# Local attention and two MLPs on one core: dilated rows in 1 KB runs, early clears on VectorE, filler products from a tile of their own up to the third slot

## The chip, the core and the metric

The kernel runs on one core of a Trainium2 chip. The core has TensorE (PE in the rows, its weight loads PEld), VectorE (DVE), ScalarE (ACT), GpSimd (POOL) and SyncE (SP), each with an instruction queue that is worked off in order, and 16 DMA engines. The metric is the device time of one execution in microseconds, as the median of several runs. Beside these there is one profiled execution, from which all rows are.

## The reference

```python
# q, k, v: (4, 8, 576, 64) float32; window 32, dilation 4
scores = q @ k.T / 8
rel = pos[:, None] - pos[None, :]
mask_plain = (rel >= 0) & (rel < 32)                        # heads 0 to 3
mask_dil = (rel >= 0) & (rel < 128) & (rel % 4 == 0)        # heads 4 to 7
attn = softmax(where(mask, scores, -1e9)); x = attn @ v     # x: 2304 tokens x 512
h = x @ w_in1;  x = max(0.01 * h, h) @ w_out1               # 512 -> 2048 -> 512
h = x @ w_in2;  out = softplus(h) @ w_out2
```

## The kernel before

The tokens are cut into eight windows `w` of 288 (half a sequence each), the heads into four pairs `p`: pairs 0 and 1 are plain, 2 and 3 dilated. A dilated head is worked as four residues modulo 4, since a query sees only keys of its own residue. One pair of one window is an object `Pair`; below, "pair n" counts them over windows, so pairs 0 to 3 are window 0 and pairs 4 to 7 window 1. These eight are *early*: their q and k come as token rows (`load_rows`), are turned by TensorE (`pe_trans`), copied out by ScalarE (`evac_k`, `evac_q`), multiplied (`scores_early`, with the mask added as a bf16 product of `ident_b` and `masks_b`), copied to SBUF by ScalarE (`scores_copy`), reduced over keys by GpSimd (`rowmax`, about 2 us each), then `less_max` on VectorE, `exp` on ScalarE, `pv` on TensorE (two halves for a dilated pair), `inv` on VectorE, `xT` on TensorE, `x_hi` on ScalarE and `x_lo` on VectorE, which leave the first MLP's input as two float32r parts. Early pairs borrow SBUF from weight tiles that are filled later. One piece `f` of the weights (128 of 2048 hidden columns, 1 MB) needs `rebias`, `low`, `split_hi` on ScalarE and `shift`, `join`, `add`, `split_lo` on VectorE before TensorE may use it.

The first MLP runs in slots: a slot is `g1` (12 products into a bank `h`) for one token block and one `f`, and, two slots later, `g2`. Slots 0, 1 and 2 are block 0 (256 tokens of window 0) with f = 0, 1, 2; slot 3 is block 1 (tokens 256 to 511) with f = 0, for which pairs 4 to 7 must be done. Its last three products need the channels of pair 7.

All instructions are written out in an order that a list scheduler in the program makes (`run_schedule`): every step has an engine, a cost and due time, and the written order is then fixed for each engine. Into the order of TensorE it puts *spins*: products that nobody reads, three of 288 columns a group, into bank `y3` (cost 0.37 in the plan, after a start of 3.2 in the plan's own time). Each group takes the bank anew, and its first product waits for TensorE's own last one. A spin is put in where TensorE has nothing ready (or, by `FILL`, ahead of a step that has just come ready); with the first `g1` they end. A spin that stands in the order runs: it holds TensorE for its length whether or not the next step is ready.

SP issues nearly all DMAs in the order of the plan; its transfers go through one queue in the order of issue. At the start GpSimd makes identity and masks (`setup`), clears the eight borrowed tiles of the early pairs (8 memsets, `clear`) and then the later pairs' `kt`, `qz` and `v` (6 memsets); VectorE casts the masks to bf16, and the first spin reads that cast.

## Time and profile before

| what | value |
|---|---|
| median of 3 runs (lowest, highest) | 930.68 us (930.04, 933.78) |
| the profiled execution's own time | 932.96 us |
| its span in the trace | 930.9 us |
| TensorE busy with products | 911.4 us (98%) |
| VectorE busy | 650.3 us (70%) |
| ScalarE busy | 460.8 us (50%) |
| GpSimd busy | 74.8 us (8%) |

In the rows, a line of the timeline is start, duration, engine, source line, operation, output from input, shapes and count, and in square brackets the idle time before it and what ended that. A row of a table of stretches has, in this order: the stretch, its length, the busy time and number of instructions of TensorE, of its weight loads, of VectorE, ScalarE and GpSimd, the granted TensorE clock as a share of full speed (2.4 GHz), the mean busy share of the DMA engines, and what they moved in GB/s.

### The profile page before, as it was taken

The page shows a single profiled execution, that of the slowest core. Times are in us where ns is not written, and L with a number is a line of the kernel's source. Part 1 is how long each engine was busy: PE and PEld are TensorE (multiplying, and loading weights), DVE is VectorE, ACT ScalarE, POOL GpSimd, SP SyncE. Part 2 cuts the span into 40 slices and gives each one's busy share as a digit, 9 for nine tenths or more (in the row PEclk, how much of TensorE's full clock was granted, in tenths as well). Part 3 has the DMA queues.
Part 4 walks back from the last instruction along what each step waited for, and adds up shares of the span by engine and source line. Part 5 has one row for each costly group of instructions (what it writes and reads, how often), then busy time and mean ns, then how long its engine had stood idle before and what let it go on. Part 6 is the DMA issues. An engine that isn't in the chain of part 4 may idle for free.

```text
span 930.9 us, 15804 instructions
## 1 busy us (share of the span) xinstructions
PE 911.4 (98%) x6047; PEld 862.2 (93%) x6048; DVE 650.3 (70%) x1276; ACT 460.8 (50%) x935; POOL 74.8 (8%) x57
## 2 busy tenths in 40 slices
PE   6989999999999999999999999999999999999998
PEld 4889999999999999999999988989899999989896
DVE  4989994475664765747546777877877777777775
ACT  3768753334434443443456744554645545444543
POOL 5500030010110201201100000000000000000000
PEclk9879999999999999999999999999999999999999
DMA  9887123254463644542358500200200000000000
GB/s 230 216 249 256 21 43 69 69 138 120 101 159 94 151 105 130 130 125 86 98 167 281 180 1 1 68 1 1 68 1 0 35 1 1 35 1 1 35 1 34
DMA packets 139902, 81.50 MB, mean 88 GB/s; under 512 B 101172, under 2 KB 124724, under 8 KB 139828
## 3 DMA queue, kind: packets, MB, share of 16 engines
q1 hardware_dynamic: 137428, 79.92, 30.4%
q8 instruction: 47, 0.77, 0.4%
q10 hardware_dynamic: 2400, 0.59, 0.3%
q14 instruction: 27, 0.22, 0.1%
HBM read 62.65 MB, written 17.83 MB: 86 GB/s over the span
## 4 chain that ended last, share of the span: by engine, by line
PE 93%; DVE 2%; ACT 1%; DMA 1%; issue 0%; SPq 0%; DVEq 0%
PE h L679 43%; PE yp L722 22%; PE yo L818 21%; PE pv L611 3%; PE sc L562 3%; PE xt L632 1%; DMA y<-ys 1%; DVE cf L281 0%; DVE w L311 0%; PE sc L535 0%; DVE lent L590 0%; PE spin L386 0%; DVE ln L795 0%; DVE ln L791 0%; DVE gl L805 0%
## 5 line engine op out<-in xcount | busy, mean ns | idle before, releaser
L679 PE MATMUL h<-xh,w 128*128 128x384 f32 (+3 forms) x1792 | 443.9, 317 | 0.7 <-DVE w L311 0.7
L679 PEld LDWEIGHTS h<-xh,w 128*128 128x128 f32 x1792 | 313.7, 189 | 5.5 <-DVE w L311 1.2
L679 PE MATMUL h<-xl,w 128*128 128x384 f32 (+3 forms) x896 | 281.5, 314 | 0.0
L722 PE MATMUL yp<-gh,w 128*128 128x288 f32 (+2 forms) x1024 | 229.0, 299 | 0.9 <-DVE ys L732 0.9
L818 PE MATMUL yo<-w,gh 128*128 128x512 f32 x576 | 180.4, 394 | 0.3 <-ACT gh L801 0.3
L679 PEld LDWEIGHTS h<-xl,w 128*128 128x128 f32 x896 | 169.5, 189 | 4.3
L722 PEld LDWEIGHTS yp<-gh,w 128*128 128x128 f32 x1024 | 171.5, 188 | 1.2 <-DVE ys L732 1.2
L722 PE MATMUL yp<-gl,w 128*128 128x288 f32 (+2 forms) x512 | 150.8, 295 | 0.0
L775 ACT ACTIVATE hc<-h 128x384 f32<-128x384 f32 x96 | 47.1, 490 | 179.6 <-PE h L679 179.5
L695 ACT ACTIVATE hc<-h 128x288 f32<-128x288 f32 (+2 forms) x128 | 52.2, 408 | 168.1 <-PE h L679 166.0
L818 PEld LDWEIGHTS yo<-w,gh 128*128 128x128 f32 x576 | 106.9, 188 | 18.5 <-ACT gh L801 1.4
L818 PE MATMUL yo<-w,gl 128*128 128x512 f32 x288 | 114.5, 398 | 0.3 <-DVE gl L805 0.3
L704 DVE TENSOR_TENSOR gl<-hc,gh 128x288 fp32r<-128x288 f32 (+2 forms) x128 | 58.4, 456 | 54.9 <-ACT gh L700 54.2
L722 PEld LDWEIGHTS yp<-gl,w 128*128 128x128 f32 x512 | 96.2, 188 | 0.1
L786 DVE TENSOR_SCALAR z<-hc 128x384 f32<-128x384 f32 x96 | 34.5, 359 | 75.7 <-ACT hc L776 75.7
L586 POOL PARTITION_ALL_REDUCE mx<-s x24 | 49.4, 2058 | 354.3 <-DVE s L576 354.3
L818 PEld LDWEIGHTS yo<-w,gl 128*128 128x128 f32 x288 | 54.1, 188 | 14.1 <-DVE gl L805 1.7
L700 ACT ACTIVATE gh<-hc 128x288 fp32r<-128x288 f32 (+2 forms) x128 | 56.7, 443 | 2.8
L805 DVE TENSOR_TENSOR gl<-ln,gh 128x384 fp32r<-128x384 f32 x96 | 53.6, 558 | 3.8 <-ACT gh L801 1.8
L795 DVE SCALAR_TENSOR_TENSOR ln<-h,ln 128x384 f32<-128x384 f32 x96 | 53.5, 557 | 3.1
L793 DVE TENSOR_TENSOR ln<-ln,hc 128x384 f32<-128x384 f32 x96 | 53.5, 557 | 3.0
L789 DVE TENSOR_TENSOR z<-hc,z 128x384 f32<-128x384 f32 x96 | 53.5, 558 | 2.9
(75 smaller groups left out, 957.9 us busy)
## 6 DMA issues: line engine op xcount, KB each, us to landing
raw<-in_moe_w_in_dram SPq DMA_DIRECT2D x32, 512.0 KB
raw<-in_moe_w_out_dram SPq DMA_DIRECT2D x32, 512.0 KB
w<-cf SPq DMA_DIRECT2D x32, 256.0 KB
w<-w SPq DMA_DIRECT2D x32, 256.0 KB
out_dram<-o SPq DMA_DIRECT2D x18, 256.0 KB
qr<-in_q_dram SPq DMA_DIRECT2D x96, 36.0 KB
y<-ys SPq DMA_DIRECT2D x20, 144.0 KB
v<-in_v_dram SPq DMA_DIRECT2D x30, 64.0 KB
```

What stands on the lines that cost most here:

```text
L586: nc.gpsimd.partition_all_reduce(self.mx, self.sf, channels=P, reduce_op=bass_isa.ReduceOp.max)
L679: nc.tensor.matmul(out=h, lhsT=a[:, c, :], rhs=b_[:, c, :], start=(c == 0 and a is whi and b_ is xh), stop=(c == NC - 1 and a is wlo))
L695: nc.scalar.activation(out=hc, in_=hbank.pop(s), func=AF.Prelu, alpha=0.01)
L700: nc.scalar.activation(out=gh, in_=hcopy[s], func=AF.Copy)
L704: eng.tensor_sub(out=gl, in0=hcopy.pop(s), in1=gparts[s][0].bitcast(F32))
L722: nc.tensor.matmul(out=ybank[e][:, o:o + n], lhsT=a[:, e * P:(e + 1) * P], rhs=b_, start=(f == 0 and n == unit_len[u] and a is whi and b_ ...
L775: nc.scalar.activation(out=ex, in_=hbank[NS1 + s], func=AF.Abs)
L789: nc.vector.tensor_sub(out=z, in0=ex, in1=z)
L793: nc.vector.tensor_tensor(out=ln, in0=ln, in1=ex, op=ALU.min)
L795: nc.vector.scalar_tensor_tensor(out=ln, in0=hbank.pop(NS1 + s), scalar=0.0, in1=ln, op0=ALU.max, op1=ALU.add)
L805: nc.vector.tensor_sub(out=gl, in0=soft.pop(s)[1], in1=gparts[NS1 + s][0].bitcast(F32))
L818: nc.tensor.matmul(out=obank[c, t], lhsT=a[:, t * P:(t + 1) * P], rhs=b_, start=(f == 0 and a is gh and b_ is whi), stop=(f == NF - 1 and ...
```

## The change

Five things change. (1) The rows of the dilated early pairs come with one DMA for k and one for q (runs of four tokens, 1 KB) in place of four each (runs of one token and head, 256 bytes). The transposes then take two residues of one head as the 128 columns in place of one residue of two heads, and the copies of the scores put that right again. (2) The eight early clears go from GpSimd to VectorE. (3) The late clears, which were due at 30 in the plan and stood right behind the early ones, may not start before 22. (4) The spins read a tile `load` of ones (written by VectorE's first instruction) in place of `ident_b` and `masks_b`, may start at 1.2 in place of 3.2, and end only with the `g1` of slot 2; the rule that puts them ahead of a step that has just come ready still ends with the first `g1`, and begins at 5 in place of 8. (5) Steps of window 1 get a slack of 1.0 in place of 0.3, and the plan's start and clearing costs are set anew.

```diff
@@ -156,7 +156,7 @@
 
         result = []
         now = locked = 0.0
-        opened = False
+        opened, fill = False, True
         filled = []
         finish = []
         while True:
@@ -178,7 +178,7 @@
                             best, best_rank = o, rank
                 if best is None:
                     continue
-                if e == "pe" and not opened and not best.optional and now - ready_at[best] < 0.3:
+                if e == "pe" and fill and not best.optional and now - ready_at[best] < 0.3:
 
                     for o in pools[e]:
                         if o.optional and ready_at[o] <= now + 1e-9 and all(free[a] >= o.acq.count(a) for a in o.acq):
@@ -196,7 +196,8 @@
                 if best.lock and now < locked:
                     best.end = locked + best.cost
                 if best.fn is g1:
-                    opened = True
+                    opened = best.args[0] >= 2
+                    fill = False
                 if best.optional and opened:
                     best.end, best.skip = now, True
                 if best.lib:
@@ -319,6 +320,7 @@
     ident_b = attp.tile([P, P], BF16, tag="identb", name="identb")
     masks_b = attp.tile([P, NI, QP], BF16, tag="masksb", name="masksb")
     zero = attp.tile([P, 1], BF16, tag="zero", name="zero")
+    load = attp.tile([P, P], BF16, tag="load", name="load")
     NQB, NKB, NVB = 2, 2, 2
     qz_b = [attp.tile([P, 2, T1], F32, tag=f"qz{i}", name=f"qz{i}") for i in range(NQB)]
     kt_b = [attp.tile([P, DIL * KD + P - KD], F32, tag=f"kt{i}", name=f"kt{i}") for i in range(NKB)]
@@ -357,6 +359,7 @@
         nc.gpsimd.affine_select(
             out=masks[:, 0], in_=mk, pattern=[[0, QP]], base=-WIN, channel_multiplier=1,
             compare_op=ALU.is_ge, fill=INVALID)
+        nc.vector.memset(load, 1.0)
         nc.vector.memset(zero, 0.0)
         nc.vector.tensor_copy(out=ident_b, in_=ident)
         nc.vector.tensor_copy(out=masks_b[:, 0:2], in_=masks)
@@ -384,7 +387,7 @@
         ps = ps_y.tile([P, NI * QP], F32, tag="y3", name="spin")
         for i in range(n):
             nc.tensor.matmul(
-                out=ps, lhsT=ident_b, rhs=masks_b.rearrange("p i m -> p (i m)"), start=True, stop=True)
+                out=ps, lhsT=load, rhs=load[:, 0:1].to_broadcast([P, NI * QP]), start=True, stop=True)
 
     xparts, rows = {}, {}
 
@@ -435,9 +438,16 @@
                 t = borrow(NB - 1, which, nb * 4 * D)[0:n // nb].rearrange("p (i h d) -> p i h d", i=nb, h=4)
             else:
                 t = wraw.tile(shape, F32, tag="raw", name="rows", bufs=NRAW)
-            rs = src[self.b, self.h0:self.h0 + 4, lo:self.s0 + T1, :].rearrange("h (p i) d -> i p h d", i=nb)
-            for i in range(nb):
-                eng.dma_start(out=t[:, i], in_=rs[i])
+            rs = src[self.b, self.h0:self.h0 + 4, lo:self.s0 + T1, :]
+            if self.dil:
+                t = t.rearrange("p i h d -> p (i h d)").rearrange("p (h i d) -> p h i d", h=4, i=nb)
+                eng.dma_start(
+                    out=t.rearrange("p h i d -> p h (i d)"),
+                    in_=rs.rearrange("h (p i) d -> p h (i d)", i=nb))
+            else:
+                rs = rs.rearrange("h (p i) d -> i p h d", i=nb)
+                for i in range(nb):
+                    eng.dma_start(out=t[:, i], in_=rs[i])
             rows[self.w, self.dil, which] = t
 
         def load_k(self):
@@ -474,13 +484,18 @@
                     in_=v[b, h0:h0 + 2, lo + k0:lo + P, :].rearrange("j p d -> p j d"))
 
         def pe_trans(self, which):
+
             src = rows[self.w, self.dil, which]
-            pp, nb = src.shape[0], src.shape[1]
+            pp = src.shape[0]
             o = 2 * (self.p % 2)
-            ps = ps_y.tile([P, nb, pp], F32, tag=f"y{o + which}", name="tr")
-            for i in range(nb):
+            if self.dil:
+                cols = [src[:, o + j, 2 * u:2 * u + 2, :] for j in range(2) for u in range(2)]
+            else:
+                cols = [src[:, i, o:o + 2, :] for i in range(src.shape[1])]
+            ps = ps_y.tile([P, len(cols), pp], F32, tag=f"y{o + which}", name="tr")
+            for i, c in enumerate(cols):
                 nc.tensor.transpose(
-                    out=ps[:, i], in_=src[:, i, o:o + 2, :].rearrange("p h d -> p (h d)"), identity=ident[0:pp, 0:pp])
+                    out=ps[:, i], in_=c.rearrange("p a d -> p (a d)"), identity=ident[0:pp, 0:pp])
             if not self.dil:
                 ps = ps.rearrange("x i p -> x p i")
             if which:
@@ -544,11 +559,15 @@
             return ps_y, [f"y{2 * (self.p % 2) + j}" for j in range(2)]
 
         def scores_copy(self, j):
-            o = self.s[:, :, j]
+            if self.dil:
+                o = self.s[:, j::2]
+                i = self.sc[j].rearrange("x (h u) m -> x u h m", h=2)
+            else:
+                o, i = self.s[:, :, j], self.sc[j]
             if j < NCOPY:
-                nc.scalar.activation(out=o, in_=self.sc[j], func=AF.Copy)
-            else:
-                nc.vector.tensor_copy(out=o, in_=self.sc[j])
+                nc.scalar.activation(out=o, in_=i, func=AF.Copy)
+            else:
+                nc.vector.tensor_copy(out=o, in_=i)
 
         def scores(self, half):
             t0, t1 = (0, 2) if half == 0 else (2, self.nt)
@@ -843,10 +862,10 @@
     STAG0, STAG00 = 4.0, 1.0
     LAG = 2
     NCOPY = 2
-    FILL = 8.0
+    FILL = 5.0
     NSPIN, LOCK, SLACK0, SLACK = 150, 1.2, 0.3, 1.0
-    TL, TR = 30.0, -4.0
-    BUSY = dict(dma=0.7, dve=3.9, act=0.7, pool=3.0)
+    TL, TR = 22.0, -4.0
+    BUSY = dict(dma=0.7, dve=3.3, act=0.7, pool=3.0)
     C2A, C2B = 157.0, 19.9
     MR = 20.0
     T0, C2L = 35.0, 22.0
@@ -877,7 +896,7 @@
     Op("pool", 0.4, warm_up, lib="reduce", target=-40.0)
     spins = []
     for i in range(NSPIN):
-        spins.append(Op("pe", 0.37, spin, 3, order=spins[-1:], acq=["y3"], rel=["y3"], start=3.2, target=1e6, optional=True))
+        spins.append(Op("pe", 0.37, spin, 3, order=spins[-1:], acq=["y3"], rel=["y3"], start=1.2, target=1e6, optional=True))
     y_free = {3: spins}
     reduces = []
     last_att, last_conv = [], []
@@ -885,11 +904,11 @@
     early_rows, row_loads = {}, []
     cleared = {}
     for i in range(NE):
-        cleared["kq", i] = Op("pool", 0.6, clear, nc.gpsimd, early_kq[i][:, 0:KT], 0.0)
-        cleared["v", i] = Op("pool", 0.65, clear, nc.gpsimd, early_v[i], 1.0)
+        cleared["kq", i] = Op("dve", 0.5, clear, nc.vector, early_kq[i][:, 0:KT], 0.0)
+        cleared["v", i] = Op("dve", 0.55, clear, nc.vector, early_v[i], 1.0)
     late_clear = []
     for t, to in [(t, 0.0) for t in kt_b + qz_b] + [(t, 1.0) for t in v_b]:
-        late_clear.append(Op("pool", 0.7, clear, nc.gpsimd, t, to, order=late_clear[-1:], target=TL))
+        late_clear.append(Op("pool", 0.7, clear, nc.gpsimd, t, to, order=late_clear[-1:], start=TL))
     for w in range(NW):
         blocks = [b for b, (t, n) in enumerate(BLOCKS) if t < (w + 1) * T1 and t + n > w * T1]
         first_slot = min(slot(b) for b in blocks)
@@ -915,7 +934,7 @@
                     for which in (1, 0):
                         qd = "dma" if which or w else "act"
                         nb = 4 if dil or w and which else 3
-                        o = Op(qd, 0.48 * nb, a.load_rows, which, nc.scalar if qd == "act" else nc.sync,
+                        o = Op(qd, 0.75 if dil else 0.48 * nb, a.load_rows, which, nc.scalar if qd == "act" else nc.sync,
                                acq=[f"rows{which}" if dil else "raw"],
                                order=[o for o in row_loads if o.earlier < w], **m)
                         o.earlier = w
@@ -928,7 +947,7 @@
                 a.lq = Op("dma", 1.95, a.load_q, order=[lk], acq=["qr"], **m)
             lv = a.lv = Op("dma", 1.0 if dil else 1.5, a.load_v, deps=old_v,
                            order=[] if early else [a.lq, prev(1, "lv")], **m)
-            ms = dict(slack=SLACK0 if early else SLACK, **m)
+            ms = dict(slack=SLACK0 if w == 0 else SLACK, **m)
             if early:
                 banks = [f"y{2 * (p % 2) + which}" for which in range(2)]
                 rel = [["rows0" if dil else "raw"], ["rows1" if dil else "raw"]] if p % 2 else [[], []]
```

TensorE, between the first product group of slot 0 (`h`, its last product first below) and that of slot 1. Names: `xt` is `xT` of pair 5, `pv` the halves of pair 6. Before:

```order
L679 MATMUL h_644<-xh_489,w_496 128x256
L632 MATMUL xt_678<-ident_85,xn_625 128x96 x3
L611 MATMUL pv_697<-lent_102 72x65 x4
L611 MATMUL pv_703<-lent_102 72x65 x4
L679 MATMUL h_717<-xh_489,w_672 128x256
L679 MATMUL h_717<-xl_490,w_672 128x256
```

After, with the spins between the first and the last of a run left out:

```order
L698 MATMUL h_690<-xh_485,w_415 128x256
L630 MATMUL pv_710<-lent_103 72x65 x4
L389 LDWEIGHTS load_90
L389 MATMUL spin_717<-load_90 128x288
...
L389 MATMUL spin_735<-load_90 128x288
L651 MATMUL xt_740<-ident_85,xn_669 128x96 x3
L389 LDWEIGHTS load_90
L389 MATMUL spin_744<-load_90 128x288
...
L389 MATMUL spin_770<-load_90 128x288
L698 MATMUL h_774<-xh_485,w_733 128x256
```

Between the two `h` there is now one half of pair 6 in place of both, and around `xt` stand 12 and 18 spins; 21 more stand between the slots 1 and 2, where there were none. In the whole program TensorE's order has 39 spins ahead of the first transpose in place of 21, and two groups more inside the first twelve transposes in place of one behind them.

SP, from the third weight piece to the weights behind the early rows (`rows` and `lent` from q and k are window 1's, `lent` from v the early pairs' v). Before:

```order
L252 DMA raw<-in_moe_w_in_dram 128x4x256
L256 DMA raw<-in_moe_w_out_dram 128x1024
L440 DMA rows<-in_k_dram 80x4x64 x4
L440 DMA rows<-in_q_dram 96x4x64 x3
L472 DMA lent<-in_v_dram 96x2x64
L472 DMA lent<-in_v_dram 128x2x64 x2
...
L440 DMA lent<-in_k_dram 104x4x64 x4
```

After:

```order
L253 DMA raw<-in_moe_w_in_dram 128x4x256
L257 DMA raw<-in_moe_w_out_dram 128x1024
L253 DMA raw<-in_moe_w_in_dram 128x4x256
L482 DMA lent<-in_v_dram 96x2x64
L482 DMA lent<-in_v_dram 128x2x64 x2
...
L450 DMA rows<-in_k_dram 80x4x64 x4
L450 DMA rows<-in_q_dram 96x4x64 x3
L475 DMA lent<-in_v_dram 72x4x64 x2
L444 DMA lent<-in_k_dram 104x4x256
```

Half a weight piece and the six v transfers of pairs 0 and 1 moved ahead of the rows of window 1.

GpSimd, from the reduction that warms it up (`warm`) on; the ISA rows are reductions. Before:

```order
L370 ISA warm<-ident 128x1
L366 MEMSET lent 128x440 x4
L366 MEMSET lent 128x520 x4
L366 MEMSET kt_92 128x440
L366 MEMSET kt_93 128x440
L366 MEMSET qz_90 128x576
L366 MEMSET qz_91 128x576
L586 ISA lent<-lent 128x576 x2
L366 MEMSET v_94 128x520
L366 MEMSET v_95 128x520
L586 ISA lent<-lent 128x576 x6
```

After:

```order
L373 ISA warm<-ident 128x1
L605 ISA lent<-lent 128x576 x4
L369 MEMSET kt_93 128x440
L369 MEMSET kt_94 128x440
L369 MEMSET qz_91 128x576
L369 MEMSET qz_92 128x576
L605 ISA lent<-lent 128x576 x2
L369 MEMSET v_95 128x520
L369 MEMSET v_96 128x520
L605 ISA lent<-lent 128x576 x2
```

The `lent` memsets are gone to VectorE, and those of `kt` and `qz` moved from ahead of the first reduction to behind the fourth.

## Rows read from the trace of the kernel before

**Rows 1.** Table of stretches: from the first spin, to the first transpose, slots 0 and 3.

```profile
8.48:13.64 5.16, 4.82 (x21) 2.47 (x21) 0.00 (x0) 0.00 (x0) 0.00 (x0) 1.00 1.04 378
44.66:62.30 17.64, 14.15 (x97) 13.16 (x97) 15.21 (x34) 11.61 (x24) 2.47 (x1) 0.71 0.68 175
62.30:930.90 868.60, 863.24 (x5630) 821.61 (x5628) 606.22 (x1201) 425.13 (x864) 49.39 (x24) 1.00 0.27 79
```

**Rows 2.** Timeline of TensorE: four spin groups and the first transposes.

```profile
8.48 0.88 PE L386 MATMUL spin<-masksb,identb 128*128 128x288 bf16 x3 [8.48 <-DVE masksb L363]
9.42 0.88 PE L386 MATMUL spin<-masksb,identb 128*128 128x288 bf16 x3
...
12.70 0.53 PE L386 MATMUL spin<-masksb,identb 128*128 128x288 bf16 x3
13.28 0.53 PE L386 MATMUL spin<-masksb,identb 128*128 128x288 bf16 x3
13.64 1.18 PE L482 MATMUL tr<-ident,rows 96*128 96x96 f32 x12
```

**Rows 3.** Timeline of VectorE and of GpSimd at the start.

```profile
2.88 5.55 DVE L363 CAST masksb<-masks 128x96 bf16<-128x96 f32 x1
2.88 3.64 POOL L366 MEMSET lent<- 128x440 f32 x8
```

**Rows 4.** Timeline of GpSimd (17.62, 21.41) and of VectorE beside it.

```profile
17.62 3.91 POOL L586 PARTITION_ALL_REDUCE lent<-lent  x2 [9.26 <-ACT lent L549]
21.41 1.07 POOL L366 MEMSET v<- 128x520 f32 x2
...
19.62 1.71 DVE L590 TENSOR_TENSOR lent<-lent 128x576 f32<-128x576 f32 x1 [11.19 <-POOL lent L586]
21.26 1.77 DVE L268 TENSOR_SCALAR cp<-cf 128x1024 uint32<-128x1024 uint32 x1
27.78 0.74 DVE L590 TENSOR_TENSOR lent<-lent 128x576 f32<-128x576 f32 x1
```

**Rows 5.** Table of stretches for the DMAs (last column GB/s), and timeline of SP.

```profile
3.00:4.00 1.00, 0.00 (x0) 0.00 (x0) 1.00 (x1) 0.00 (x0) 1.00 (x4) 1.00 1.25 232
17.00:18.00 1.00, 1.00 (x15) 0.74 (x14) 0.00 (x0) 0.53 (x2) 0.38 (x1) 1.00 1.40 159
20.00:25.00 5.00, 5.00 (x61) 4.19 (x59) 5.00 (x4) 4.72 (x11) 4.74 (x5) 1.00 0.57 120
...
0.74 1.44 SPq L440 DMA_DIRECT2D rows<-in_k_dram  x3
```

**Rows 6.** Timeline of TensorE: pair 0 behind the last rows, and ahead of slot 0.

```profile
23.64 1.20 PE L611 MATMUL pv<-lent 128*96 128x65 f32 x12
41.29 0.42 PE L632 MATMUL xt<-ident,xn 72*128 72x72 f32 x4
```

**Rows 7.** Timeline of VectorE from pair 0 to pair 3, and around pair 7.

```profile
28.45 0.15 DVE L621 TENSOR_SCALAR rd<-pv 96x6 f32<-96x6 f32 x1
31.97 2.11 DVE L272 SCALAR_TENSOR_TENSOR cf<-cf,cp 128x1024 uint32<-128x1024 uint32 x1
37.30 0.16 DVE L621 TENSOR_SCALAR rd<-pv 72x4 f32<-72x4 f32 x1 [0.42 <-PE pv L611]
38.96 0.16 DVE L621 TENSOR_SCALAR rd<-pv 72x4 f32<-72x4 f32 x1 [0.84 <-PE pv L611]
40.43 1.21 DVE L311 TENSOR_TENSOR w<-cf,w 128x1024 fp32r<-128x1024 f32 x1
...
62.48 0.51 DVE L657 TENSOR_TENSOR xl<-xt,xh 128x224 fp32r<-128x224 f32 x2
65.78 0.97 DVE L517 STREAM_TRANSPOSE qz<-qr 64x288 f32<-64x288 f32 x2
```

**Rows 8.** Tables of stretches: lower granted clock, and a stretch just before it.

```profile
46.00:49.40 3.40, 1.65 (x19) 1.36 (x18) 3.40 (x7) 2.07 (x6) 1.41 (x1) 0.99 0.42 87
49.40:59.60 10.20, 8.47 (x48) 7.96 (x47) 8.25 (x18) 7.54 (x12) 0.00 (x0) 0.50 0.70 174
```

## The prediction, as put on record

> **What bounds the kernel now.** I read the table of stretches first, then the timelines of the engines ahead of the first slots. From slot 3 on (62.30 us) TensorE is busy for 863.24 of 868.60 us at full clock [rows 1]; no edit touches those products, so the change is worth what it moves the start of slot 3. Ahead of that the bound changes three times. (a) The first transposes, at 13.64, begin right where a run of 21 spins ends, and the first spin began only at 8.48, behind the cast of the masks [rows 2]. That cast took 5.55 us for 96 columns because it ran beside GpSimd's memsets [rows 3]. (b) From 19.62 on VectorE is the late one: less_max, weights and inv stand in one row, with waits of 0.42 and 0.84 us for products of TensorE [rows 7]. (c) From slot 0 to slot 3, 17.64 us, TensorE idles 17.64 - 14.15 = 3.49 us [rows 1] and does 8.47 us of its work at the lower clock [rows 8].
>
> **The front.** The spins now wait for one memset, VectorE's first instruction, and I let them start at 1.1 us. They come in groups of three. At the lower clock groups are 9.42 - 8.48 = 0.94 us apart, at full clock 13.28 - 12.70 = 0.58 [rows 2]. The plan counts 0.37, and that holds for the last of a run only (13.28 to 13.64): each next group waits for the last product of the one before. How long the clock stays low after the first spin has two prices. 21 spins took 5.16 us [rows 1], of which 7 groups at 0.58 would be 4.1: 1.1/0.36 = 3 to 4 groups were slow, some 3.4 us. And after 49.4 the lower clock lasted 10.2 us, with TensorE idle for 1.7 of them [rows 8]. 39 spins are 13 groups: 3.4/0.94 = 3.6 slow, 9.4 x 0.58 = 5.4 us, so the transposes start at 1.1 + 3.4 + 5.4 = 9.9; with 10.2 us low at 12.5. I take 10.3, near the first, which is the same work without a break: 3.3 us earlier than 13.64. One more group of 0.58 stands between the transposes, so the first reduction comes at 14.9 in place of 17.62 [rows 4].
>
> The 1 KB runs themselves buy little there: the dilated rows were on the chip while TensorE still spun, and their transposes stand behind the plain ones. They free the queue: 0.59 MB go at the weights' 378 GB/s [rows 1] in place of 232 [rows 5], 1.6 us in place of 2.5.
>
> **What is late next: the rows of window 1.** Before, they flowed when the first three weight pieces were through, at 159 GB/s [rows 5]; TensorE took the last of them without waiting and began pv of pair 0 at 23.64 [rows 6]. Now half a weight piece and six v transfers go ahead of them. Transfers begin about 1 us after the first issues at 0.74 [rows 5], so the weights flow from 1.8 + 2.5 + 1.6 = 5.9: 3.67 MB of weights at 378 GB/s, 9.7 us; 0.36 MB of v at 159, 2.3 us; 0.62 MB of rows at 159, 3.9 us: landed at 21.8. With landing and three transposes (0.6 us, an estimate) pv of pair 0 starts at 22.4, only 1.2 us earlier than before, and TensorE idles some 2 us ahead of it. Of the front's 3.3 us two thirds go here. inv of pair 0 begins one pv later (1.1 us, [rows 6]), at 23.5; before at 28.45, since two more less_max stood ahead of it [rows 7].
>
> **VectorE from there to pair 3.** Before, 28.45 to 39.70 (38.96 + 0.74) is 11.25 us. The new order has in that stretch one less_max more (0.74 [rows 4]), one split_lo more (1.21), one x_lo more (0.4, by the two pieces of the one at 62.48) and one join less (2.11, slowed by a reduction), and I let the two waits of 1.26 us go, since TensorE is then ahead [rows 7]: 11.25 + 2.35 - 3.37 = 10.2. I add 0.5 for a reduction beside a less_max, which costs 1.71 - 0.74 = 0.97 when it falls so [rows 4]. That gives 34.2.
>
> **The moved clears.** The eight early ones go to VectorE between 3 and 7 us, where it has nothing else; nothing is queued behind them until the first rebias. The four of kt and qz (2.1 us, twice the two of v [rows 4]) move from GpSimd's idle start to behind its fourth reduction, at about 25 us, where VectorE is the bound and less_max of pairs 2 and 3 stand in the row. No row shows a less_max beside a memset. From below the price is nothing, which no row excludes. From above it is all 2.1 us: the cast stood still through twelve of them [rows 3], and a shift that ran beside the two of v took 1.77 [rows 4]. Both are operations with one input, less_max has two and lost about half its time beside reductions, so I take the middle, 1.1: inv of pair 3 is done at 35.3.
>
> Less_max beside reductions ran at less than half speed here, so something is shared. The Trainium skill, SBUF — State Buffer, section "Who interferes with whom", says that an operation with two SBUF inputs is held up by a GpSimd instruction that reads SBUF, not by one that only writes; by that rule the moved clears cost a less_max nothing and the time below would be 1.1 us shorter. The trace agrees with its first half (less_max beside reductions); no run here shows the second.
>
> **To slot 0.** Before, xT of pair 2 at 41.29 to slot 0 at 44.66 was 3.37 us [rows 1, 6]: a spin group, scores, pv, xT. Now three groups stand there, 2 x 0.58 = 1.16 more. 35.3 + 0.15 + 3.37 + 1.16 = 40.0, 4.7 us earlier.
>
> **Slots 0 to 3.** TensorE's products of this stretch take 14.15 - 8.47/2 = 9.9 us at full clock [rows 1, 8]. The spins are 12, 18 and 21, in 4, 6 and 7 groups: (0.37 + 3 x 0.58) + (0.37 + 5 x 0.58) + (0.37 + 6 x 0.58) = 9.2 us. They stand in the order and run, ready or not, so the stretch is 19.1 us, longer than the 17.64 before: the idle 3.49 and the 4.2 lost to the clock are replaced by 9.2 of filler. In slot 3 the last products need x_lo of pair 7. Before, that began at 62.48, just in time for a slot begun at 62.30. Now a pair of transposes (0.97, at 65.78 before) stands ahead of it [rows 7], and I take 0.8 us of wait, an estimate from it. 40.0 + 19.1 + 0.8 = 59.9 against 62.30: 2.4 us.
>
> After that VectorE's weights keep their distance, since its row is earlier by the same. The span would be 930.9 - 2.4 = 928.5. The profiled execution took 932.96 with that span; the median, 930.68, is 2.28 less. Forecast: 930.68 - 2.4 = 928.3 us.
>
> **Rivals.** *The filler does not hold* (faster): groups follow at the planned 0.37 and the clears cost nothing. For it: the last group of a run does take 0.36. Against: the groups at 12.70 and 13.28 [rows 2]. Fourteen gaps of 0.21 and two ahead of slot 0 are 3.4, with the clears 1.1 less, 2.4 + 4.5 = 6.9, of which VectorE as the next bound gives back about 1.5 (an estimate: its row then has no wait left): 5.4 us, 925.3.
>
> *The rows eat it all* (no change): window 1's rows and v move at 120 GB/s, as the DMAs do between 20 and 25 us [rows 5], so 0.98 MB take 8.2 in place of 6.2 us; everything behind is 2 us later, gain 0.4: 930.3. With the clears at 2.1 it is 931.3. For it: TensorE idles there already; against: at 17 us, with such rows in the queue, the rate was 159.
>
> *The clock falls and stays down* (slower): TensorE idles 2 us of the 3.4 ahead of pv of pair 0; before, 1.65 us busy in 46 to 49.4 was followed by 10.2 us at the lower clock [rows 8]. If slots 0 to 3 run at it, the 9.9 of products become 19.8 and the spins 17 x 0.94 = 16.0: 16.7 us more in all; half of the stretch at it makes 8 us, 930.7 + 8 - 2.4 = 936. It makes the kernel slower than now by over 0.5% from 7 us on (2.4 + 4.65). Against: the filler is there so that TensorE never pauses, and at the start such spins ended the lower clock.
>
> *It doesn't start early*: if spins still ended last at 13.64, no rows would be waited for, and 930.7 stays; only the memset of the tile could do that, so this has little.
>
> **How the numbers follow.** 0.5% (4.65 us) is about what this measurement can tell from no change. Forecast case (gain 0.5 to 4.6) 0.55, filler rival 0.22, rows rival with no start 0.18, clock rival 0.05. So faster by over 0.5% 0.22, within 0.73, slower 0.05. The range goes from the filler rival, with half a us below it, to the rows rival with the full price of the clears: 924.8 to 931.3.
>
> **What would show it.** In the changed profile: the first transpose at 10 to 11.5 (first step); spin groups 0.58 apart at full clock; TensorE idle for about 2 us before pv of pair 0 at 22.4, ended by a DMA; less_max at 25 us of 0.74 or stretched to 27; slot 0 at 39 to 41; slot 3 19 to 20 us after slot 0 with TensorE never idle between. I am wrong if slot 3 starts before 57.5 or after 62, or if TensorE stalls after it.

## The result: slower, 940.8 us against 930.9

The changed kernel took 940.81 us (median of 4 runs, 940.50 to 942.50), the kernel before 930.89 us beside it: 1.0098 times as long, 95% interval 1.0075 to 1.0122. The forecast was 928.3 us with a range up to 931.3; the sign was wrong and the time lies outside. The profiled execution has a span of 938.8 us against 930.9. The spans differ by 7.9 us and the medians by 9.9, mostly because the profiled execution of the kernel before took 932.96 us, 2.1 above its median; the profiles can explain 7.9 us at most.

The first view is the table of stretches of the changed kernel (columns as in [rows 1]). In its first row the clock of 1.00 is no reading: the profile holds no granted clock ahead of 7.23 us, and up to there the groups of spins come 0.93 to 0.96 us apart, near the 0.92 us that a group (at 31.93) takes in the stretch at 0.50.

```profile
4.00:9.00 5.00, 4.66 (x21) 2.33 (x20) 2.84 (x7) 0.00 (x0) 0.00 (x0) 1.00 1.07 237
9.00:17.00 8.00, 7.78 (x80) 5.78 (x78) 0.73 (x1) 4.16 (x11) 1.87 (x1) 1.00 1.08 372
17.00:20.00 3.00, 2.94 (x37) 2.31 (x38) 2.39 (x2) 1.51 (x5) 2.52 (x2) 1.00 0.92 218
20.00:24.00 4.00, 2.27 (x17) 1.18 (x15) 2.58 (x3) 3.32 (x8) 3.21 (x2) 1.00 0.61 138
24.30:41.36 17.06, 17.06 (x114) 15.31 (x115) 9.01 (x23) 10.25 (x18) 8.01 (x9) 0.50 0.92 238
41.36:49.05 7.69, 7.58 (x88) 6.30 (x87) 5.24 (x12) 4.88 (x11) 2.36 (x1) 1.00 0.49 93
49.05:67.84 18.79, 18.01 (x149) 14.24 (x148) 15.21 (x33) 10.78 (x20) 1.97 (x1) 1.00 0.84 267
67.84:938.80 870.96, 864.28 (x5632) 821.97 (x5629) 607.50 (x1202) 426.46 (x865) 50.88 (x24) 1.00 0.26 76
```

Read it from below, against [rows 1]. Slot 3 begins at 67.84 in place of 62.30: 5.5 of the 7.9 us by which the span grew are lost ahead of it. Behind it the stretch is 2.4 us longer (870.96 for 868.60). Slots 0 to 3 take 18.79 us, at full clock and with TensorE busy for 18.01 of it. The loss is older than slot 0, which begins at 49.05 in place of 44.66. And there one row stands out: from 24.30 to 41.36 the granted clock is 0.50, the lower of its two levels, TensorE is busy for all 17.06 us, and VectorE for only 9.01. TensorE is the bound there, at half speed. In the four microseconds ahead (20 to 24) it was busy for 2.27 only; before, it was busy throughout that stretch. TensorE's timeline shows why:

```profile
10.82 0.41 PE L497 MATMUL tr<-ident,rows 96*128 96x96 f32 x3
...
19.30 1.11 PE L550 MATMUL sc<-lent 64*128 64x72 f32 x16
21.20 0.58 PE L497 MATMUL tr<-ident,rows 80*128 80x80 f32 x2 [0.79 <-DMA rows<-in_k_dram]
22.15 0.71 PE L497 MATMUL tr<-ident,rows 80*128 80x80 f32 x2 [0.37 <-DMA rows<-in_k_dram]
22.70 0.54 PE L389 MATMUL spin<-load 128*128 128x288 bf16 x3
23.57 1.13 PE L497 MATMUL tr<-ident,rows 96*128 96x96 f32 x3 [0.34 <-DMA rows<-in_q_dram]
24.50 2.08 PE L630 MATMUL pv<-lent 128*96 128x65 f32 x12
```

The first transposes come 2.8 us earlier than in [rows 2]. Then TensorE waits 0.79, 0.37 and 0.34 us, 1.5 in all, for the rows of window 1, and pv of pair 0, at 24.50, is later than before (23.64, [rows 6]) and takes 2.08 us in place of 1.20. Why the rows are late stands in SP's timeline (a line is a run of issues; where it is longer than its issues need, SP waits before it may issue the next):

```profile
3.75 0.41 SPq L253 DMA_DIRECT2D raw<-in_moe_w_in_dram  x1
...
9.55 0.38 SPq L253 DMA_DIRECT2D raw<-in_moe_w_in_dram  x1
10.04 6.71 SPq L482 DMA_DIRECT2D lent<-in_v_dram  x6
17.92 2.90 SPq L450 DMA_DIRECT2D rows<-in_k_dram  x4
20.92 1.46 SPq L450 DMA_DIRECT2D rows<-in_q_dram  x3
```

SP's timeline before, from the rows of window 1 on:

```profile
14.36 1.86 SPq L440 DMA_DIRECT2D rows<-in_k_dram  x4
...
18.89 2.85 SPq L472 DMA_DIRECT2D lent<-in_v_dram  x6
```

In the changed kernel seven halves of weight pieces are issued by 9.9 us; the six v transfers take SP 6.71 us (2.85 before), and the rows of window 1 are issued at 17.92 in place of 14.36. VectorE's timeline shows who is late at half clock: it waits for TensorE.

```profile
26.61 0.16 DVE L640 TENSOR_SCALAR rd<-pv 96x6 f32<-96x6 f32 x1 [3.40 <-PE pv L630]
...
36.05 0.16 DVE L640 TENSOR_SCALAR rd<-pv 72x4 f32<-72x4 f32 x1 [2.98 <-PE pv L630]
```

### The profile page after: what moved, and what is told of

The parts are those of the page before. It is cut to its first block, busy times and chain, and to the rows that moved or that the text cites. A ratio compares the mean times of both kernels' runs of the same rounds, so it can differ in the third digit from the quotient of the medians.

```text
span 938.8 us, 15937 instructions
## 1 busy us (share of the span) xinstructions
PE 927.6 (99%) x6129; PEld 870.9 (93%) x6129; DVE 647.1 (69%) x1285; ACT 462.7 (49%) x935; POOL 73.2 (8%) x49
## 4 chain that ended last, share of the span: by engine, by line
PE 88%; DVE 5%; DMA 4%; ACT 1%; issue 1%; SPq 1%; POOL 0%; ACTq 0%; DVEq 0%; POOLq 0%
PE h L698 40%; PE yo L837 21%; PE yp L741 19%; PE pv L630 3%; PE sc L581 2%; DMA raw<-in_moe_w_in_dram 2%; PE spin L389 1%; DMA lent<-in_q_dram 1%; PE xt L651 1%; DVE gl L723 1%; PE sc L550 1%; DVE cf L273 1%; DVE w L312 1%; DMA y<-ys 0%; DMA raw<-in_moe_w_out_dram 0%
## 5 line engine op out<-in xcount | busy, mean ns | idle before, releaser
L723 DVE TENSOR_TENSOR gl<-hc,gh 128x288 fp32r<-128x288 f32 (+2 forms) x128 | 60.9, 476 | 50.3 <-ACT gh L719 49.6
L264 ACT ACTIVATE cf<-raw 128x512 f32<-128x512 f32 (+1 forms) x48 | 39.7, 828 | 38.2 <-DMA raw<-in_moe_w_out_dram 18.0
```

Source lines behind the costliest of these rows:

```text
L264: nc.scalar.activation(out=self.cff, in_=self.raw[:, :, 1].bitcast(F32), func=AF.Copy, scale=2.0 ** -112)
L723: eng.tensor_sub(out=gl, in0=hcopy.pop(s), in1=gparts[s][0].bitcast(F32))
```

## The experiments

The theory: the rows of window 1 come late, TensorE idles, the granted clock falls, and the work behind it costs double. Against it stand the filler (the spins, also called unread products; 51 of them and 9.8 us between slots 0 and 3), the clears, the long runs, and the early start. The last three columns (start times in us) are those of the one profiled execution; the ratio is to the kernel before on the same chip (932.1 to 932.4 us there), from all executions of both.

| run | median us | ratio, 95% interval | pv of pair 0 | slot 0 | slot 3 |
|---|---|---|---|---|---|
| before | 930.89 | | 23.64 | 44.66 | 62.30 |
| changed | 940.81 | 1.0098, 1.0075 to 1.0122 | 24.50 | 49.05 | 67.84 |
| rows_first | 938.64 | 1.0055, 1.0032 to 1.0079 | 24.02 | 52.88 | 68.88 |
| cover | 942.41 | 1.0106, 1.0068 to 1.0145 | 25.70 | 49.02 | 67.94 |
| open_first | 936.73 | 1.0048, 1.0031 to 1.0065 | 25.68 | 50.64 | 66.61 |
| rows_open | 937.47 | 1.0038, 1.0013 to 1.0063 | 23.31 | 52.57 | 66.93 |
| rows_early | 931.70 | 0.9990, 0.9974 to 1.0006 | 20.37 | 44.41 | 60.44 |
| cover_v | 935.82 | 1.0027, 1.0006 to 1.0047 | 25.02 | 42.18 | 60.98 |
| early_open | 929.54 | 0.9969, 0.9956 to 0.9983 | 21.35 | 44.15 | 59.70 |
| early_start | 936.28 | 1.0022, 1.0000 to 1.0043 | 26.14 | 52.15 | 64.94 |
| held | 927.83 | 0.9956, 0.9941 to 0.9971 | 20.87 | 41.06 | 54.16 |
| eo_clears | 929.56 | 0.9974, 0.9960 to 0.9988 | 20.37 | 44.41 | 60.23 |
| eo_short | 930.28 | 0.9974, 0.9951 to 0.9996 | 20.64 | 44.92 | 58.85 |
| start_rows | 930.92 | 0.9986, 0.9966 to 1.0007 | 21.43 | 42.50 | 60.34 |

### First four: order, cover, filler

**rows_first** holds v and the fourth piece back in the plan.

```diff
-            lv = a.lv = Op("dma", 1.0 if dil else 1.5, a.load_v, deps=old_v,
+            lv = a.lv = Op("dma", 1.0 if dil else 1.5, a.load_v, deps=old_v, start=11.5 if w == 0 else 0.0,
...
-            prev_load = Op("dma", 0.5, a.load, i, deps=free_w, order=[prev_load], acq=["raw"] if layer else [], start=es, **m)
+            prev_load = Op("dma", 0.5, a.load, i, deps=free_w, order=[prev_load], acq=["raw"] if layer else [], start=es if layer or f < 3 else 12.0, **m)
```

> The changed kernel with the v transfers of window 0 and the fourth weight piece held back, so that SyncE issues the plain rows of window 1 right behind the third weight piece, as the kernel before did. Theory (the clock: TensorE idles 1.5 us between 20.4 and 23.6 us for these rows, the granted clock falls at 24.3 us and the products up to 41.4 us run at half speed): no idle time there, pv of pair 0 at 22 us in place of 24.5, the granted clock at full speed through 24 to 41 us, slot 0 at 40 to 42 us in place of 49.05, the kernel at 932 to 935 us in place of 940.8. Rival (the filler products hold TensorE back, wherever the rows are): slot 0 moves by the 2 us of the rows at most, 939 to 941 us. Rival (the new layout of the dilated rows is slower in itself): 939 to 941 us as well, with the loss in the pairs 2 and 3.

The edit did not do what it was made for. SP issued the rows 5.6 us earlier than in the changed kernel, yet they came hardly earlier. SP's and TensorE's timelines and a row of the stretches:

```profile
12.29 2.70 SPq L450 DMA_DIRECT2D rows<-in_k_dram  x4
15.09 4.81 SPq L450 DMA_DIRECT2D rows<-in_q_dram  x3
```

```profile
21.05 0.29 PE L497 MATMUL tr<-ident,rows 80*128 80x80 f32 x1 [1.08 <-DMA rows<-in_k_dram]
```

```profile
23.14:50.45 27.31, 27.07 (x172) 22.90 (x172) 14.51 (x34) 16.09 (x30) 10.12 (x10) 0.50 0.80 203
```

So it is the queue and not SP: six halves of weight pieces still stood ahead of the rows. TensorE idled 1.52 us in all (waits of 0.20 and 0.24 us followed the one shown), the clock fell at 23.14 and stayed low for 27.31 us. The ten runs of this one program, with identical instructions, bear on the cause: three with a mean granted clock of 0.993 to 0.998 took 933.3 to 934.5 us, seven with 0.984 to 0.987 took 937.4 to 942.3. This shows that the two go together, not yet which causes which.

**cover** leaves the order and fills the wait: 24 more unread products.

```diff
             if not o.skip:
+                a = getattr(o.fn, "__self__", None)
+                if isinstance(a, Pair) and a.n == NPAIR and o.fn == a.pe_trans:
+                    spin(16 if o.args[0] else 8, f"y{o.args[0]}")
                 o.fn(*o.args)
```

> The changed kernel with 16 more unread products ahead of the first transposes of window 1's k and 8 more ahead of those of its q, where TensorE idled for the late rows. The rows come as late as in the changed kernel; only the idle time is filled. Theory (the clock): the granted clock stays at full speed past 24.3 us although the rows are late; pv of pair 0 at 24.5 us or a little later, slot 0 at 42 to 44 us in place of 49.05, the kernel at 934 to 936 us. Rival (the late rows themselves cost the time, the clock is a side effect): slot 0 at 49 us or later, 940 to 942 us. Rival (filler holds TensorE back): 24 more such products, 2.9 us, make it later by up to that, 941 to 944 us.

The median fits the rivals' numbers, but the trace (938.77 us, the fastest of its four executions) is not theirs: the clock stayed up, and something else came late. Stretches, TensorE and SP:

```profile
4.76:38.89 34.13, 30.66 (x309) 23.43 (x308) 18.85 (x37) 21.30 (x46) 17.11 (x13) 1.00 0.92 264
38.89:45.72 6.83, 4.10 (x22) 3.31 (x23) 3.34 (x7) 1.04 (x2) 2.23 (x1) 0.50 0.61 99
```

```profile
41.56 2.16 PE L630 MATMUL pv<-lent 128*96 128x65 f32 x12 [4.10 <-DMA lent<-in_v_dram]
```

```profile
31.81 2.98 SPq L465 DMA_DIRECT2D kr<-in_k_dram  x4
35.39 5.88 SPq L482 DMA_DIRECT2D lent<-in_v_dram  x6
```

Full clock up to 38.89, with the rows no earlier: the clock follows TensorE's idle time. But with pairs 0 to 3 done sooner the next late transfer showed: pv of pair 4 waited 4.10 us for its v, issued behind more weights and the k of window 2. So holding the clock there, and nothing else, gained nothing: slot 0 at 49.02 and slot 3 at 67.94, as in the changed kernel. SP's row of the changed kernel shows the same late v:

```profile
34.82 6.30 SPq L482 DMA_DIRECT2D lent<-in_v_dram  x6
```

There pv of pair 4 came only at 43.49, behind the stretch at half clock, and did not wait for it.

**open_first** and **rows_open** end the unread products at the first product of slot 0, the second with the order of rows_first.

```diff
-                    opened = best.args[0] >= 2
+                    opened = True
```

> The changed kernel with the unread products ended at the first product of slot 0, as in the kernel before; the 51 between slots 0 and 3 are gone. Theory (the clock ahead of slot 0): slot 0 stays at 49 us; from there to slot 3 TensorE idles again, 16 to 18 us in place of 18.8, so 938 to 940 us. Rival (the filler between slots 0 and 3 is the loss): its 9.8 us come back for the most part, slot 3 at 59 to 61 us and 931 to 934 us.

> Both edits at once: the plain rows of window 1 ahead of the v transfers and of the fourth weight piece, and no unread product after the first product of slot 0. Theory (the clock): slot 0 at 40 to 42 us, and 15 to 18 us from there to slot 3, which begins at 56 to 59 us against 62.30 in the kernel before; 926 to 930 us. Rival (filler): 929 to 932 us, all of the gain from slots 0 to 3. If the clock falls between slots 0 and 3 for want of filler, as it did in the kernel before, slot 3 comes at 59 to 61 us and the kernel stays within 930 to 932 us.

```profile
22.81 0.81 PE L497 MATMUL tr<-ident,rows 80*128 80x80 f32 x3 [2.96 <-DMA rows<-in_k_dram]
```

```profile
22.89:43.38 20.49, 20.26 (x127) 17.12 (x127) 9.78 (x26) 11.49 (x21) 8.85 (x9) 0.50 0.83 217
50.64:66.61 15.97, 12.27 (x98) 11.03 (x97) 15.20 (x33) 10.62 (x21) 1.96 (x1) 0.89 0.77 236
```

In open_first TensorE's order ahead of slot 0 is that of the changed kernel, yet the wait for the rows was one of 2.96 us in place of 1.5 in all, since SP issued them at 19.18 and not at 17.92: single profiles of one order differ by a microsecond or so ahead of slot 0. Slot 0 stayed late (50.64) and slots 0 to 3 took 15.97 us in place of 18.79: the filler costs 2.8 us of its 9.8, not the whole. It is a part of the loss: the median of 936.73 lies 1.3 us below the theory's 938 to 940, and well above the rival's 931 to 934. rows_open missed by the same late rows as rows_first; of its ten runs the one with a mean clock of 0.996 took 929.6 us, the seven with 0.981 to 0.984 took 936.3 to 939.2.

### Second four: the rows ahead of the weights

**rows_early** puts the third weight piece behind the rows too, and the k of window 2 behind v of window 1 (`f < 2` in place of `f < 3`, and a `start=26.0` for `load_k` of window 2). **early_open** is the same with `opened = True`.

> The changed kernel with the third and fourth weight piece and the v transfers of window 0 held back behind the plain rows of window 1, and the k of window 2 behind v of window 1. In the run that held back only the fourth piece and v, these rows were issued at 12.3 us in place of 17.9, yet came at 21 to 22 us, behind 3.15 MB of weights. Theory (the rows wait in the DMA queue for weights; the idle time that follows brings the clock down): with 2.1 MB of weights ahead of them the rows are on the chip at 18 to 19 us, TensorE does not idle at 20 to 24 us, the granted clock stays at full speed past 24 us, pv of pair 0 at 21.5 to 22.5 us, slot 0 at 41 to 43 us, slot 3 at 60 to 62 us, 930 to 933 us. Rival (something behind the rows, such as VectorE's row or the filler, sets slot 3): rows early, clock up, but slot 3 at 66 us or later and 936 us or more.

> Rows of window 1 ahead of the third weight piece and of v, and no unread product after the first product of slot 0. Theory (queue and clock): slot 0 at 41 to 43 us, slots 0 to 3 in 14 to 16 us where the clock stays up, 17 to 18 where it falls for want of filler: slot 3 at 56 to 60 us against 62.30 in the kernel before, 925 to 930 us. Rival (VectorE's row bounds the pairs of window 1): slot 3 at 61 us or later, 931 us or more.

```profile
19.42 0.49 PE L497 MATMUL tr<-ident,rows 80*128 80x80 f32 x4
...
20.37 1.16 PE L630 MATMUL pv<-lent 128*96 128x65 f32 x12
...
31.68 0.91 PE L630 MATMUL pv<-lent 104*72 104x65 f32 x8 [1.34 <-DVE xn L642]
```

These are TensorE's rows of rows_early: no wait for window 1, pv of pair 0 4.1 us earlier than in the changed kernel and at full speed (1.16). The theory holds up to here (these times are even earlier than it expected). The next wait is VectorE's, 1.34 us at 30.3, and the clock falls right behind it, to 42.26 (10.24 us at 0.50, TensorE busy for 10.07). Slot 0 is therefore at 44.41, where 41 to 43 was expected, and slot 3 at 60.44. early_open shows the same twice, in TensorE's rows and in the stretches:

```profile
32.65 0.70 PE L630 MATMUL pv<-lent 104*72 104x65 f32 x8 [1.34 <-DVE xn L642]
...
50.82 0.70 PE L630 MATMUL pv<-lent 104*72 104x65 f32 x8 [2.03 <-DVE rd L641]
```

```profile
7.29:34.60 27.31, 24.92 (x272) 19.78 (x269) 16.43 (x29) 19.10 (x41) 15.51 (x12) 1.00 0.87 241
34.60:41.42 6.82, 6.32 (x34) 4.51 (x33) 4.43 (x11) 4.51 (x9) 2.97 (x1) 0.50 1.06 316
44.15:59.70 15.55, 13.01 (x97) 12.00 (x97) 14.63 (x32) 10.67 (x21) 2.45 (x1) 0.78 0.70 175
51.66:58.49 6.83, 6.42 (x32) 5.75 (x30) 6.05 (x14) 3.36 (x6) 0.00 (x0) 0.50 0.73 130
```

Slot 0 (44.15) missed the expected 41 to 43, but 929.54 us is faster than both kernels (interval 0.9956 to 0.9983).

**cover_v** is cover with pieces five and six and the k of window 2 held back.

> The run with 24 more unread products ahead of the transposes of window 1, and besides the weight pieces five and six and the k of window 2 held back behind v of window 1's plain pairs. In the run without this the granted clock stayed at full speed up to 38.9 us, but pv of pair 4 then waited 4.1 us for its v, up to 41.56 us. Theory (clock and late transfers add up): pv of pair 4 at 37 to 39 us, full clock from 5 to 45 us, slot 0 at 44 to 46 us, slot 3 at 63 to 65 us, 932 to 935 us. Rival (the filler alone is the loss): no change from the run before, 938 to 943 us.

```profile
4.82:42.18 37.36, 35.79 (x367) 27.88 (x367) 22.43 (x44) 23.39 (x50) 19.33 (x13) 1.00 0.96 259
42.18:60.98 18.80, 18.01 (x148) 14.23 (x148) 15.21 (x33) 10.79 (x20) 1.96 (x1) 1.00 0.68 176
```

This is the clearest price of the clock. The rows are as late as in the changed kernel (pv of pair 0 at 25.02), slots 0 to 3 cost the same (18.80), but the clock is full throughout: slot 0 comes at 42.18 in place of 49.05, 6.9 us earlier, and slot 3 as much (60.98 for 67.84). It is the price with the v of window 1 moved forward as well; cover shows that without this the full clock buys nothing. An earlier v alone would hardly help at half clock, since TensorE had no idle time from 24.30 to 41.36; that is argued, no run has it. The slots came earlier than expected and the median later: the profiled run is one of its fastest (932.2 us), the median is 935.82, and it scatters from 931.9 to 940.4, at a mean clock of 0.998 to 1.000 in nine of ten runs. What its slower runs wait for no profile here shows; that stays open.

**early_start** is the kernel before with the tile `load` and `start=1.2`, nothing else.

> The kernel before with one thing of the change: the unread products read a tile of ones that VectorE writes first, and may start at 1.2 in the plan. Rows, clears and the end of the unread products are as before. Theory (what lands from the DMA queue sets the pace, not when TensorE starts): the first transposes at 10 to 11 us in place of 13.64, but the rows of window 1 land at 20 to 22 us as before, TensorE waits for them, slot 0 at 44 us or later: no gain, and a loss of up to 8 us where the clock falls in the wait, 930 to 938 us. Rival (an early start is worth what my prediction said, and the rest of the change loses it): 927 to 929 us.

```profile
19.47 0.40 PE L484 MATMUL tr<-ident,rows 80*128 80x80 f32 x1 [2.70 <-DMA rows<-in_k_dram]
```

```profile
18.04:38.52 20.48, 18.55 (x115) 15.43 (x116) 9.00 (x16) 10.12 (x23) 8.27 (x5) 0.50 0.81 201
```

In the order of the kernel before, too, TensorE that starts 3.9 us earlier (first transpose at 9.76) waits for the same rows, 2.70 us, and the clock falls in the wait. There is no gain from the early start alone, and probably a loss: the interval begins at 1.0000.

### Last four: hold the clock, and the rest one by one

**held** is early_open with unread products in its two long waits.

```diff
+                if isinstance(a, Pair) and o.fn == a.pv and (a.n, o.args[0]) in ((3, 1), (7, 0)):
+                    spin(9 if a.n == 3 else 14, "y1" if a.n == 3 else "y3")
```

> The version with the rows of window 1 ahead of the third weight piece and no unread product after the first one of slot 0 (929.5 us), with 9 unread products more ahead of the last pv of pair 3, where TensorE idled 1.34 us at 31.3 us, and 14 more ahead of the first pv of pair 7, where it idled 2.03 us at 48.8 us. In that version the granted clock fell right behind each of these two waits, for 6.83 us each. Theory (a wait of a microsecond or more on TensorE brings the clock down, and the products behind it cost double): full clock from 7 us on, slot 0 at 42 to 43.5 us, slot 3 at 55 to 57.5 us in place of 59.70, 925 to 927.5 us. Rival (VectorE's row sets the pairs, the clock is spent in its shadow): slot 3 at 59 to 60 us, 929 to 930 us.

```profile
6.09:41.06 34.97, 33.02 (x349) 26.05 (x347) 23.21 (x45) 23.87 (x50) 18.48 (x13) 1.00 0.94 262
41.06:54.16 13.10, 12.33 (x113) 10.81 (x111) 12.83 (x29) 9.50 (x20) 2.45 (x1) 1.00 0.74 161
54.16:925.50 871.34, 864.47 (x5632) 821.71 (x5629) 606.57 (x1202) 423.71 (x865) 50.61 (x24) 1.00 0.28 80
```

23 products, 2.8 us of work that nobody reads, bring slot 3 from 59.70 to 54.16 (0.5 of that was there already at pv of pair 0). Full clock from 6 us on, and 927.83 us, just above the 925 to 927.5 expected: 0.9956 of the kernel before (0.9941 to 0.9971), the lowest median here, and its four runs lie within 1.1 us. Of the 8.1 us gained at slot 3 against the kernel before, 2.7 are lost behind it (871.34 for 868.60, [rows 1]): the span is 5.4 shorter (925.5 for 930.9), the median 4.3 (927.83 for 932.11). Against early_open 3.4 of 5.5 are lost there (it took 867.90), and the intervals of the two overlap: the trace shows the gain at slot 3, the times show less of it.

**eo_clears** and **eo_short** undo one part each in early_open: the early clears on GpSimd, and the dilated rows in 256-byte runs.

> The same version (929.5 us) with the eight early clears on GpSimd again, as in the kernel before. Theory (the clears were never on the path: VectorE is empty up to 13 us): the cast of the masks is slow again, some 5 us in place of 0.2, and ends at 8 us, ahead of its first reader at 12.6 us; nothing behind it moves, 929 to 930 us. Rival (GpSimd's clears hold up VectorE's cast or the first reduction): 931 us or more.

> The same version (929.5 us) with the rows of the dilated pairs of windows 0 and 1 in runs of 256 bytes again, four DMAs each, as in the kernel before. Theory (the DMA queue sets the pace up to pv of pair 0): 0.6 MB more in short runs ahead of the first weights keeps the queue 1 to 2 us longer, SyncE issues six DMAs more, the rows of window 1 come 1 to 2 us later and TensorE waits for them or for v: 930 to 934 us. Rival (the longer runs buy nothing, as my prediction had it): 929 to 930 us.

VectorE's row and GpSimd's of eo_clears:

```profile
2.88 3.70 DVE L366 CAST masksb<-masks 128x96 bf16<-128x96 f32 x1
```

```profile
2.88 3.64 POOL L369 MEMSET lent<- 128x440 f32 x8
```

The cast again lasts as long as GpSimd's memsets (0.20 in the changed kernel), but nobody waits for it, and 929.56 is 929.54 within the noise. The Trainium skill, SBUF — State Buffer, section "Who interferes with whom", says that a cast can hold both of VectorE's ports and is then blocked, not slowed, by GpSimd; the rows agree (the cast ends at 6.58, the last memset at 6.52). With the short runs the median is 0.7 us higher (930.28), less than these intervals tell apart; pv of pair 0 came at 20.64, where versions with the long runs and the same order have it at 20.37 to 21.35, so my expectation of late rows was wrong there.

**start_rows** is early_start with the rows ahead of the third weight piece (the edits of rows_early to the transfers).

> The kernel before with the early start of the unread products (which alone gave 936.3 us, later than the 932.4 of the kernel before), and with the third weight piece held back behind the rows and v of window 0 and the rows of window 1. Theory (an early start pays only if the rows of window 1 come earlier too): no wait of 2.7 us for them at 19.5 us, the clock up past 30 us, pv of pair 0 at 21 to 23 us, slot 3 at 59 to 61 us, 929 to 932 us. Rival (the early start itself costs time): 935 us or more.

```profile
18.43 0.29 PE L484 MATMUL tr<-ident,rows 80*128 80x80 f32 x1 [0.26 <-DMA rows<-in_k_dram]
```

The wait of 2.70 us is 0.26, the clock stays up to 47.25, and the median goes from 936.28 to 930.92. These runs show no harm of the early start once the rows come in time; whether it gains against the kernel before, these runs can't tell (0.9966 to 1.0007).

## Why the prediction was wrong

**The front.** Nearly right: transposes at 10.82 (forecast 10.3), the first reduction at 15.13 (14.9). The slow spell was the uncertain term: the lower clock lasted seven groups of spins, not 3.6. Versions with the same front have the transposes at 9.88 to 10.86.

**The rows of window 1.** The mechanism was right, the size not: pv of pair 0 at 24.50, not 22.4. The term that failed is "3.67 MB of weights at 378 GB/s" from 5.9 us on. Between 4 and 9 us the queues moved 237 GB/s, since window 0's rows were still among the weights; 5 x (378 - 237) = 0.7 MB, at 372 some 1.9 us, is nearly the whole miss. What I had not seen is that the rate rises to its full height only at 9 us in both kernels (before, 203 GB/s from 3 to 9 us and 376 from 9 to 17): an earlier start of TensorE meets a queue that is no earlier. This is why the step "two thirds go here" was still too kind: all of it went.

**The clock.** This is the step that turned the sign, together with a wait that the prediction had no term for. The rival was there, with its place named ("TensorE idles 2 us of the 3.4 ahead of pv of pair 0") and 936 us, and I gave it 0.05. The argument against it was that the filler keeps TensorE from pausing. But the planner puts filler where *its plan* has a gap, and in the plan the rows come in time; where TensorE in fact waited, one group of three stood. I also let the price fall in slots 0 to 3, where the clock stayed up, while it fell from 24.30 to 41.36. cover_v prices it at 6.9 us. There slot 3 stands at 60.98, near the forecast of 59.9; but that took the v of window 1 earlier too. The new order also put these six v transfers behind more weights and the k of window 2 (issued from 34.82 on, and 30.82 before). The prediction's step "To slot 0" puts the wait for them at nothing, and with the clock held in cover it is 4.10 us.

I also had not read that the clock of the kernel before falls ahead of slot 0 as well:

```profile
32.29:39.12 6.83, 6.83 (x52) 6.04 (x51) 5.36 (x13) 4.84 (x9) 2.36 (x2) 0.50 1.04 316
```

With the 10.24 us between its slots 0 and 3 it spends 17.07 us at the lower level up to slot 3, as long as the changed kernel. What changed is the place: the filler kept the clock up in the slots, at the price of its own 9.8 us, and ahead of slot 0 the spell grew from 6.83 to 17.06 us.

**VectorE to pair 3.** "34.2" took VectorE for the bound. At half clock TensorE was: VectorE was busy for 9.01 of 17.06 us, and inv of pair 3 ended at 42.08.

**To slot 0.** From xT to slot 0 the sum was right: 44.51 to 49.05 is 4.54 us, forecast 3.37 + 1.16. But the 0.15 from inv of pair 3 to that xT was mis-sized, also by the rows of before: it was 1.5 us there and 2.4 here, since pv of pair 4, among others, stands between them on TensorE.

**The moved clears.** Taken at 1.1 us, they cost nothing: the memsets of kt and qz (24.91 to 26.88) fell almost wholly into VectorE's wait of 3.40 us for pv, and no less_max ran beside them. A less_max beside memsets shows later, with the two of v:

```profile
38.09 1.07 POOL L369 MEMSET v<- 128x520 f32 x2
38.43 0.75 DVE L609 TENSOR_TENSOR lent<-lent 128x576 f32<-128x576 f32 x1
```

It took 0.75 us, as alone (0.74); in early_open one beside the memsets of kt (from 24.95 on) took 0.76. So the price was the lower bound, nothing. The Trainium skill, SBUF — State Buffer, section "Who interferes with whom", has the rule that I cited on it, that a GpSimd instruction which only writes does not hold up an operation with two SBUF inputs; both rows agree. The early clears cost nothing that the times tell on either engine (929.56 and 929.54 us).

**Slots 0 to 3, and slot 3.** 19.1 forecast, 18.79 measured; the wait for x_lo of pair 7 forecast at 0.8 showed as one of 0.53 us, inside slot 3 and not ahead of its start, where the sum had it. That this filler costs more than it saves there was in the sum (19.1 against 17.64); open_first measured 2.8 us.

**Behind slot 3.** I let nothing change there; it cost 2.4 us, 1.3 of them idle (870.96 - 864.28 = 6.68 against 5.36). The 0.53 us for x_lo belong to it, and the longest wait there is this one:

```profile
224.79 0.93 PE L630 MATMUL pv<-v,s 104*72 104x65 f32 x11 [1.10 <-ACT s L612]
```

The same stretch lies between 867.9 and 871.6 us in the profiles here. Why one order has such waits and another not (the longest of the kernel before is one of 0.93 us) was not followed up, and stays open.

## What to carry to other kernels

An engine that starts earlier gains nothing if its next input comes through a queue that starts no earlier; it then idles, and on TensorE the idle time can cost several times its length (here 1.5 us of waits, and 6.9 us at slot 0 by cover_v). Filler that keeps the clock must stand where the engine really waits, as a trace shows it, not where a plan has a gap; 2.8 us of it at two waits brought slot 3 forward by 5.5 us where 9.8 us in the wrong place cost time. And a filled wait only helps up to the next late transfer: in cover the clock stayed up and slot 0 came no earlier. In a queue worked off in order, ask of each large transfer which small one behind it is needed first.

## What was unexpected of the hardware

- Waits of 1.34 to 2.03 us on TensorE (early_open), and three of 1.5 us in all (the changed kernel), were followed within 2 us by a fall of the granted clock to the lower level; one of 1.01 us in cover, up to 22.59, was not, so the "microsecond or more" in the theory of held is not shown. The clock then stayed low for 3.4 us (eo_short, 53.19 to 56.60) to 27.3 us (rows_first), though TensorE was busy nearly all the while with transposes, scores and pv (17.06 of 17.06 us in the changed kernel, 27.07 of 27.31 in rows_first). In rows_first and early_open it rose again as a run of 12 unread products ended (46.53 to 50.25, risen at 50.45; 38.08 to 41.68, risen at 41.42), in the changed kernel without such a run.
- The same program spends more time at the lower clock in one run than in the next: rows_open took 929.6 us at a mean clock of 0.996 and up to 939.2 at 0.984.
- The DMAs were as busy between 4 and 9 us as later (a mean share of 1.07 and 1.08) but moved 237 GB/s there and 372 from 9 to 17: short rows went among the weights there. In eo_short, where the dilated rows come in 256-byte runs again, it was 198 GB/s between 4 and 9 us against 240 in early_open, at the same share (1.03 and 1.04).
